# Key sums by head on either side of the array, the first k in two loads, and narrower first units, in a fused attention and expert kernel

The kernel runs on 1 core of one Trainium2 chip. The metric is the device time of one execution in microseconds (us); lower is better.

## The reference

```python
def phi(x):                                  # polynomial sketch, r = 8, so 64 features
    a = einsum('rd,bhsd->bhsr', S1, x); b = einsum('rd,bhsd->bhsr', S2, x)
    return einsum('bhsi,bhsj->bhsij', a, b).reshape(..., 64)
q_p, k_p = phi(q), phi(k)                    # batch 4, heads 4, seq 1088, head_dim 32
kv = einsum('bhsf,bhsd->bhfd', k_p, v); z = k_p.sum(axis=2)
attn = einsum('bhsf,bhfd->bhsd', q_p, kv) / (einsum('bhsf,bhf->bhs', q_p, z)[..., None] + 1e-6)
x = attn as 4352 rows of 128                 # heads side by side
p = domain_probs / (domain_probs.sum(-1) + 1e-9)
out = sum over 4 experts of p[:, e] * (relu(x @ w1[e]) @ w2[e])   # w1: 128 x 1024
```

## The kernel before

The expert product goes chunk by chunk over the rows: 16 steps a chunk, each with `first` (hidden block: TensorE, then ScalarE and VectorE) and, two steps later, `second` (TensorE). Attention work of later rows is cut into pieces and slipped between the steps; a unit is the number of query rows handled at once. Only the first 128 rows are handled ahead of everything, in `start`. A record is one matmul instruction of the trace. A PSUM tile is what a matmul of this program writes; `f`, `h`, `o`, `den` and `num` are such tiles. `den` and `num` are the products for the denominator and the numerator of the attention; their weights, `kvz`, are written by the key division from the key sums. To turn is to transpose.

```python
    UNITS = [[P, 480, 480]] + [[384, 352, 352]] * 3          # rows of a query unit, by batch
    CHUNKS = [P, 480, 480] + [512] * 5 + [320, 256, P]       # rows of an expert chunk
    ...
    def both(out, weights, moving, **flags):                 # the two 64-column sides of the array
        for _ in range(2):
            on_side(lambda s: out[half[s], :], lambda s: weights[:, half[s]], lambda s: moving, **flags)
    ...
    def key_sum(b, p, kv, t0=0, n=NT):                       # kv and z of a pair p of heads
        for t in range(t0, t0 + n):
            both(
                kv[:, 256 * p : 256 * p + 2 * (D + 1)],
                kps[b][:, t, p, :],                          # features of both heads: 128 columns
                vx[:, t, 2 * p : 2 * p + 2].rearrange("p h d -> p (h d)"),   # v and a 1, two heads: 66
                start=(p == t == 0), stop=(t == NT - 1), skip_group_check=True,
            )

    def key_divide(b, kv):                                   # zeroes the blocks of the wrong head
        kvz = apool.tile([P, 2, 2, HP], F32, tag="kvz", bufs=2, name="kvz")
        for i in (1, 0):                                     # 1: weights of den, 0: of num
            nc.vector.tensor_tensor(out=..., in0=_ap(kv, ...), in1=_ap(own2, ...), op=ALU.mult)
        kvzs[b] = kvz
    ...
    load_rows(k, 0, "kn")                                    # all 1088 columns in one load
    load_rows(q, 0, "qn", slice(0, P))
    ...
    for _ in range(14):                                      # warm-up matmuls
        wp = psum(ps_h, "h")
        nc.tensor.matmul(wp[:, :], warm[:, 0:P], warm[:, :], start=True, stop=True)
```

## Time and profile before

| | before |
|---|---|
| time, median of the first 3 runs | 501.05 us (500.58 to 501.96) |
| span of the profiled run | 499.2 us |
| TensorE busy, granted clock (share of the full TensorE clock) | 98%, 0.999 |
| first expert matmul | 15.49 us |
| from it to the first matmul of the last chunk | 464.22 us |

The lines of the profile on which the prediction rests stand in it, below.

### The profile page before, as it was taken

Reading aid. Unit: us, or ns where it says so; the run is one execution under the profiler, and the core shown is the slowest. Engines: PE = TensorE matmul, PEld = TensorE weight load, DVE = VectorE, ACT = ScalarE, POOL = GpSimd, SP = SyncE. Lnnn points to the kernel's source line nnn. Section 1 sums busy time; section 2 is a strip of 40 time slices with the busy share of each in tenths; the row PEclk is TensorE's granted clock in tenths of the full one; section 3 lists DMA queues with packets and bytes.
Section 4 is the critical chain, followed back from the end, with each engine's and each line's share of the span. In section 5 each row is a group of like instructions: output and inputs, shape, how many; then the busy total and the mean of one; then the engine's idle time right before and its main releaser. Section 6 shows DMA issues by size and latency. Waiting matters only on the chain.

```text
span 499.2 us, 11045 instructions
## 1 busy us (share of the span) xinstructions
PE 490.8 (98%) x4442; PEld 367.8 (74%) x4442; DVE 326.5 (65%) x749; ACT 250.7 (50%) x491; POOL 229.8 (46%) x264
## 2 busy tenths in 40 slices
PE   8899999999999999999999999999999999999997
PEld 6775788777776657777777777777777777788996
DVE  5858675868667585757657646558656557665643
ACT  4543553545454454544545455445455445556662
POOL 6730333444544263444545344344555355655571
PEclk9999999999999999999999999999999999999999
DMA  7981030021002330031001100021001100110000
GB/s 203 286 293 51 1 91 1 2 85 20 1 2 85 66 91 0 1 85 22 3 1 64 43 1 1 2 85 22 2 1 53 23 1 1 43 23 2 14 3 17
DMA packets 29666, 22.36 MB, mean 45 GB/s; under 512 B 20016, under 2 KB 26800, under 8 KB 29232
## 3 DMA queue, kind: packets, MB, share of 16 engines
q1 hardware_dynamic: 29312, 21.40, 15.3%
q8 instruction: 35, 0.57, 0.5%
q10 hardware_dynamic: 304, 0.26, 0.2%
q14 instruction: 15, 0.12, 0.1%
HBM read 19.35 MB, written 2.31 MB: 43 GB/s over the span
## 4 chain that ended last, share of the span: by engine, by line
PE 96%; DVE 3%; issue 0%; ACT 0%; DVEq 0%; ACTq 0%
PE h L186 48%; PE o L186 39%; PE f L186 5%; PE den L186 2%; PE num L186 1%; PE h L176 1%; DVE qp L420 1%; DVE hid L592 1%; DVE qa L479 0%; DVE qf L469 0%; DVE qb L474 0%; DVE qf L471 0%; DVE end L657 0%; ACT hid L618 0%; ACT fs L348 0%
## 5 line engine op out<-in xcount | busy, mean ns | idle before, releaser
L592 DVE SCALAR_TENSOR_TENSOR hid<-h,hid 128x256 f32<-128x256 f32 (+6 forms) x432 | 203.7, 472 | 149.0 <-ACT hid L618 140.7
L186 PE MATMUL h<-xT,w_sb 128*64 128x512 f32 (+4 forms) x1408 | 298.7, 496 | 1.7 <-DVE xT L454 1.4
L618 ACT ACTIVATE hid<-h 128x512 f32<-128x512 f32 (+3 forms) x288 | 158.3, 550 | 202.4 <-PE h L186 169.9
L186 PE MATMUL o<-hid,w2s 128*64 128x256 f32 (+3 forms) x1152 | 220.9, 355 | 0.0
L186 PEld LDWEIGHTS h<-xT,w_sb 128*64 128x64 f32 x1408 | 149.5, 137 | 52.7 <-issue 4.7
L186 PE MATMUL o<-hid,w_sb 128*64 128x256 f32 (+3 forms) x864 | 185.0, 356 | 0.6 <-DVE end L657 0.6
L186 PEld LDWEIGHTS o<-hid,w2s 128*64 128x64 f32 x1152 | 131.5, 137 | 31.7 <-issue 0.6
L733 POOL TENSOR_TENSOR ev<-yz,sh 64x256 f32<-64x256 f32 (+3 forms) x72 | 48.6, 675 | 159.0 <-ACT sh L736 156.3
L186 PEld LDWEIGHTS o<-hid,w_sb 128*64 128x64 f32 x864 | 101.4, 137 | 21.1 <-issue 1.6
L721 POOL TENSOR_TENSOR yz<-ev 128x512 f32<-128x512 f32 (+3 forms) x36 | 42.3, 1175 | 84.1 <-ACT ev L724 83.9
L733 POOL TENSOR_TENSOR ct<-ev 128x512 f32<-128x512 f32 (+3 forms) x36 | 42.2, 1173 | 2.8
L733 POOL TENSOR_TENSOR ct<-ct,gate 128x512 f32<-128x512 f32 (+3 forms) x27 | 31.9, 1183 | 2.1
L733 POOL TENSOR_TENSOR total<-total,ct 128x512 f32<-128x512 f32 (+3 forms) x27 | 31.8, 1177 | 2.1
L420 DVE TENSOR_TENSOR qp<-qa,qb 64x352 f32<-64x352 f32 (+2 forms) x44 | 31.6, 719 | 1.0
L610 ACT ACTIVATE hid<-h 128x256 f32<-128x256 f32 x24 | 15.3, 655 | 18.7 <-PE h L186 18.2
L723 ACT COPY ev<-o 128x512 f32<-128x512 f32 (+3 forms) x36 | 19.4, 538 | 9.4 <-PE o L186 8.9
L186 PE MATMUL o<-w_sb,hid 128*64 128x128 f32 x256 | 24.0, 273 | 0.0
L186 PEld LDWEIGHTS o<-w_sb,hid 128*64 128x64 f32 x256 | 19.9, 137 | 1.7 <-issue 1.5
L724 ACT COPY ev<-o 128x512 f32<-128x512 f32 (+3 forms) x36 | 19.4, 539 | 3.0
L359 DVE TENSOR_TENSOR kp<-fs 128x256 f32<-128x256 f32 (+1 forms) x24 | 16.1, 677 | 0.0
L736 ACT COPY sh<-yz 64x256 f32<-64x256 f32 (+3 forms) x36 | 13.7, 379 | 1.4 <-POOL yz L721 0.5
L737 ACT COPY sh<-yz 64x256 f32<-64x256 f32 (+3 forms) x36 | 13.7, 380 | 0.9
(93 smaller groups left out, 250.8 us busy)
## 6 DMA issues: line engine op xcount, KB each, us to landing
w_sb<-in_moe_w_dram SPq DMA_DIRECT2D x8, 512.0 KB, 7.7
gate<-gates SPq DMA_DIRECT2D x3, 1024.0 KB, 4.9
kn<-in_k_dram SPq DMA_DIRECT2D x4, 544.0 KB, 4.1
gate<-gates SPq DMA_DIRECT2D x2, 960.0 KB, 5.4
vn<-in_v_dram SPq DMA_DIRECT2D x14, 128.0 KB, 5.0
qn<-in_q_dram SPq DMA_DIRECT2D x3, 544.0 KB, 4.1
gate<-gates SPq DMA_DIRECT2D x1, 896.0 KB
out_dram<-ob SPq DMA_DIRECT2D x12, 64.0 KB, 2.0
```

The costliest lines, as they stand in the source:

```text
L186: nc.tensor.matmul(out(s), weights(s), moving(s), **flags)
L359: eng.tensor_tensor(out=_ap(kps[b], 0, P, 256 * t0 + P * p + 64 * x, [[256, n], [32, 2], [R, 4], [1, R]]), in0=in0, in1=_ap(fss[b], 0, P, ...
L420: nc.vector.tensor_tensor(out=qp[p][64 * x : 64 * x + 64, 0:n], in0=qa[64 * p : 64 * p + 64, 0:n], in1=qb[64 * p : 64 * p + 64, 0:n], op=A ...
L592: nc.vector.scalar_tensor_tensor(out=out, in0=src, scalar=0.0, in1=in1, op0=ALU.max, op1=ALU.subtract)
L610: nc.scalar.activation(turned, src, ACTF.Relu)
L618: nc.scalar.activation(hd[:, n * j : n * j + n], hp[:, 0:n], ACTF.Relu)
L721: add = lambda out, in0, in1, op=ALU.add: nc.gpsimd.tensor_tensor(out=out, in0=in0, in1=in1, op=op)
L723: nc.scalar.copy(_ap(ev, 0, P, 0, [[2 * w, 2], [1, w]]), _ap(a0, 0, P, 0, two))
L724: nc.scalar.copy(_ap(ev, 0, P, w, [[2 * w, 2], [1, w]]), _ap(a1, 0, P, 0, two))
L733: add = lambda out, in0, in1, op=ALU.add: nc.gpsimd.tensor_tensor(out=out, in0=in0, in1=in1, op=op)
L736: nc.scalar.copy(sh[HP:P, 0:w], yz[0:HP, 0, 0:w])
L737: nc.scalar.copy(sh[0:HP, 0:w], yz[HP:P, 1, 0:w])
```

## The change

The intent: a key sum computes only what is used (33 columns of one head on each side, instead of 66 of which half are zeroed); TensorE can start on the first half of k; the start has fewer sketch matmuls and warm-ups; and the first rows come in three units of 320, so that VectorE has less to do beside the first chunk.

```diff
-    QW = 480
+    QW = 384
-    UNITS = [[P, 480, 480]] + [[384, 352, 352]] * 3
+    UNITS = [[P, 320, 320, 320]] + [[384, 352, 352]] * 3
-    CHUNKS = [P, 480, 480] + [512] * 5 + [320, 256, P]
+    CHUNKS = [P, 320, 320, 320, 384] + [512] * 4 + [448, 256, P]
 ...
-    load_rows(k, 0, "kn")
+    kn[0] = lpool.tile([P, S], F32, tag="kn", bufs=2, name="kn")
+    for r in range(2):
+        nc.sync.dma_start(
+            _ap(kn[0], 0, P, P * r, [[8 * D, 4], [1, P]]),
+            bass.AP(k.tensor, k.offset + P * r, [[G * D, P], [8 * D, 4], [1, P]]),
+        )
     load_rows(q, 0, "qn", slice(0, P))
+    vn[0] = load_v(0, (nc.sync, nc.scalar), (0, 1))
+    load_rows(k, 0, "kn", slice(1024, S))
+    load_v(0, (nc.sync, nc.scalar), (2,), vn[0])
 ...
-    vn[0] = load_v(0, (nc.sync, nc.scalar))                  # stood a few lines further down
 ...
-    for _ in range(14):
+    for _ in range(11):
 ...            # key sketch: per head 16 columns; ScalarE's copies 8 -> 4; query sketch of the start 4 tiles -> 3
     def key_sum(b, p, kv, t0=0, n=NT):
         for t in range(t0, t0 + n):
-            both(
-                kv[:, 256 * p : 256 * p + 2 * (D + 1)],
-                kps[b][:, t, p, :],
-                vx[:, t, 2 * p : 2 * p + 2].rearrange("p h d -> p (h d)"),
+            for _ in range(2):
+                on_side(
+                    lambda s: kv[half[s], (D + 1) * p : (D + 1) * (p + 1)],
+                    lambda s: kps[b][:, t, p, half[s]],
+                    lambda s: vx[:, t, 2 * p + s],
 ...
     def key_divide(b, kv):
-        for i in (1, 0):
-            nc.vector.tensor_tensor(... own2 ...)
+        for i, copy in ((1, nc.vector.tensor_copy), (0, nc.scalar.copy)):
+            for h in range(2):
+                for x in range(2):
+                    copy(
+                        _ap(kvz[b % 2], 64 * x + 32 * h, 32, HP * i + D * h, [[P, 2], [1, D]]),
+                        _ap(kv, 64 * h + 32 * x, 32, D * i, [[D + 1, 2], [1 - i, D]]),
+                    )
 ...            # hidden blocks of the narrow chunks written straight instead of turned; the
                # gates' ends and the output of those chunks addressed row by row instead
-            if i:
+            if i > NQ // 2:
                 next(to_sum, None)
```

More of the change, by code (lines that the diff above doesn't have):

```diff
@@ L93, in load_rows, with load_v @@
         nc.sync.dma_start(d[b][:, part], bass.AP(src.tensor, src.offset + b * H * S * D + c, [[G * D, P], [1, n]]))
-    def load_v(b, engines):
-        t = lpool.tile([P, H * NT * D], F32, tag="vn", name="vn")
+    def load_v(b, engines, parts=(0, 1, 2), t=None):
+        t = t or lpool.tile([P, H * NT * D], F32, tag="vn", name="vn")
         base = v.offset + b * H * S * D
         for a in range(4):
-            engines[a // 2].dma_start(
-                _ap(t, 32 * a, 32, 0, [[8 * D, H], [1, 8 * D]]),
-                bass.AP(v.tensor, base + 8 * a * D, [[G * D, 32], [S * D, H], [1, 8 * D]]),
-            )
-        for a in range(2):
+            if a // 2 in parts:
+                engines[a // 2].dma_start(
+                    _ap(t, 32 * a, 32, 0, [[8 * D, H], [1, 8 * D]]),
+                    bass.AP(v.tensor, base + 8 * a * D, [[G * D, 32], [S * D, H], [1, 8 * D]]),
+                )
+        for a in range(2 if 2 in parts else 0):
             nc.sync.dma_start(
@@ L148 @@
         nc.sync.dma_start(
-            ends[:, i, :], bass.AP(domain_probs.tensor, domain_probs.offset + t * E, [[G * E, 32], [1, 4 * E]])
+            ends[:, i, :], bass.AP(domain_probs.tensor, domain_probs.offset + t * E, [[E, 4], [G * E, 32], [1, E]])
         )
@@ L154 @@
         load_w2(e)
-    own2 = cpool.tile([P, 2], F32, name="own2")
     sk = cpool.tile([P, P], F32, name="sk")
-    sp = cpool.tile([32, 4, HP], F32, name="sp")
-    sr = cpool.tile([P, 4, 2, P], F32, name="sr")
+    sp = cpool.tile([32, 3, 2, 32], F32, name="sp")
+    sr = cpool.tile([P, 3, 2, P], F32, name="sr")
     sq = cpool.tile([P, P], F32, name="sq")
@@ L163 @@
     nc.gpsimd.memset(sq[:, :], 0.0)
-    nc.gpsimd.memset(own2[:, :], 0.0)
-    for h in range(H):
-        nc.gpsimd.memset(own2[32 * h : 32 * h + 32, h % 2 : h % 2 + 1], 1.0)
     kT = cpool.tile([P, P * NT], F32, name="kT")
@@ L171 @@
     nc.gpsimd.memset(vx[64:P, NT - 1, :, 0:D], 0.0)
-    for _ in range(14):
+    kvz = [cpool.tile([P, 2, 2, HP], F32, name=f"kvz{i}") for i in range(2)]
+    for t in kvz:
+        nc.gpsimd.memset(t[:, :, :, :], 0.0)
+    for _ in range(11):
         wp = psum(ps_h, "h")
@@ L230 @@
     for h in range(H):
-        nc.scalar.copy(
-            _ap(sk, 32 * h, 32, R2 * (h // 2) + 4 * (h % 2), [[H * R2, 2], [R, 2], [1, 4]]),
-            _ap(s_T, 0, 32, 0, [[D, 2], [4, 2], [1, 4]]),
-        )
-        nc.scalar.copy(
-            _ap(sk, 32 * h, 32, H * R + R * h, [[H * R2, 2], [1, R]]), _ap(s_T, 0, 32, R, [[D, 2], [1, R]])
-        )
-    for i in range(2):
-        for j in range(2):
-            nc.gpsimd.tensor_copy(
-                _ap(sp, 0, 32, HP * (2 * i + j), [[32, 2], [R, 4], [1, R]]),
-                _ap(s_T, 0, 32, D * j, [[4, 2], [1, 4], [0, R]]) if i else _ap(s_T, 0, 32, D * j + R, [[0, 2], [0, 4], [1, R]]),
-            )
-    for h in range(H):
-        for i in range(2):
-            nc.gpsimd.tensor_copy(
-                _ap(sr, 32 * h, 32, P * (4 * i + 2 * (h // 2)) + 32 * (h % 2), [[P, 2], [HP, 2], [1, 32]]),
-                _ap(sp, 0, 32, P * i, [[HP, 2], [32, 2], [1, 32]]),
-            )
+        nc.scalar.copy(_ap(sk, 32 * h, 32, R2 * h, [[HP, 2], [1, R2]]), _ap(s_T, 0, 32, 0, [[D, 2], [1, R2]]))
+    for i in range(3):
+        nc.gpsimd.tensor_copy(
+            _ap(sp, 0, 32, HP * i, [[32, 2], [R, 4], [1, R]]),
+            _ap(s_T, 0, 32, 4 * (i - 1) if i else R, [[D, 2]] + ([[1, 4], [0, R]] if i else [[0, 4], [1, R]])),
+        )
+    for h in range(H):
+        nc.gpsimd.tensor_copy(
+            _ap(sr, 32 * h, 32, 32 * h, [[P, 6], [1, 32]]), _ap(sp, 0, 32, 0, [[32, 6], [1, 32]])
+        )
     mask_lo = [R2 + l % R2 for l in range(32)]
@@ L313 @@
     FG = ((0, 4), (4, 4), (8, 1))
-    fss, kps, kvzs = {}, {}, {}
+    fss, kps = {}, {}
     def key_turn(b, r):
@@ L336, in key_project @@
         if gi == 0:
-            fss[b] = apool.tile([P, 4, NT, R2], F32, tag="fs", name="fs")
+            fss[b] = apool.tile([P, 2, NT, 32], F32, tag="fs", name="fs")
             kps[b] = apool.tile([P, NT, 2, P], F32, tag="kp", name="kp")
@@ L340, in key_project @@
             for i in range(2):
-                both(
-                    kf[:, HP * t : HP * t + HP],
-                    kT[:, P * (t0 + t) : P * (t0 + t + 1)],
-                    sk[:, HP * i : HP * i + HP],
-                    start=(i == 0),
-                    stop=(i == 1),
-                )
+                for _ in range(2):
+                    on_side(
+                        lambda s: _ap(kf, HP * s, HP, 32 * t, [[P, 2], [1, 32]]),
+                        lambda s: kT[:, P * (t0 + t) + HP * s : P * (t0 + t) + HP * s + HP],
+                        lambda s: sk[:, HP * i : HP * i + HP],
+                        start=(i == 0),
+                        stop=(i == 1),
+                    )
         nc.scalar.copy(
-            _ap(fss[b], 0, P, R2 * t0, [[R2, n], [R2 * NT, 4], [1, R2]]),
-            _ap(kf, 0, P, 0, [[HP, n], [R2, 4], [1, R2]]),
+            _ap(fss[b], 0, P, 32 * t0, [[32 * NT, 2], [1, 32 * n]]), _ap(kf, 0, P, 0, [[P, 2], [1, 32 * n]])
         )
     def key_product(b, t0, n, p, x, eng, kf=None):
-        if kf is None:
-            in0 = _ap(fss[b], 0, P, R2 * (NT * p + t0) + R * x, [[R2, n], [4, 2], [1, 4], [0, R]])
-        else:
-            in0 = _ap(kf, 0, P, R2 * p + R * x, [[HP, n], [4, 2], [1, 4], [0, R]])
+        src, off = (kf, P * p) if kf is not None else (fss[b], 32 * (NT * p + t0))
         eng.tensor_tensor(
-            out=_ap(kps[b], 0, P, 256 * t0 + P * p + 64 * x, [[256, n], [32, 2], [R, 4], [1, R]]),
-            in0=in0,
-            in1=_ap(fss[b], 0, P, R2 * (NT * (2 + p) + t0), [[R2, n], [R, 2], [0, 4], [1, R]]),
+            out=_ap(kps[b], 0, P, 256 * t0 + P * p + 32 * x, [[256, n], [HP, 2], [R, 4], [1, R]]),
+            in0=_ap(src, 0, P, off + 4 * x, [[32, n], [R2, 2], [1, 4], [0, R]]),
+            in1=_ap(fss[b], 0, P, 32 * (NT * p + t0) + R, [[32, n], [R2, 2], [0, 4], [1, R]]),
             op=ALU.mult,
@@ L367, in key_sum @@
         for t in range(t0, t0 + n):
-            both(
-                kv[:, 256 * p : 256 * p + 2 * (D + 1)],
-                kps[b][:, t, p, :],
-                vx[:, t, 2 * p : 2 * p + 2].rearrange("p h d -> p (h d)"),
-                start=(p == t == 0),
-                stop=(t == NT - 1),
-                skip_group_check=True,
-            )
-    def key_divide(b, kv):
-        kvz = apool.tile([P, 2, 2, HP], F32, tag="kvz", bufs=2, name="kvz")
-        for i in (1, 0):
-            nc.vector.tensor_tensor(
-                out=_ap(kvz, 0, P, HP * i, [[P, 2], [D, 2], [1, D]]),
-                in0=_ap(kv, 0, P, D * i, [[256, 2], [D + 1, 2], [1 - i, D]]),
-                in1=_ap(own2, 0, P, 0, [[0, 2], [1, 2], [0, D]]),
-                op=ALU.mult,
-            )
-        kvzs[b] = kvz
+            for _ in range(2):
+                on_side(
+                    lambda s: kv[half[s], (D + 1) * p : (D + 1) * (p + 1)],
+                    lambda s: kps[b][:, t, p, half[s]],
+                    lambda s: vx[:, t, 2 * p + s],
+                    start=(p == t == 0),
+                    stop=(t == NT - 1),
+                    skip_group_check=True,
+                )
+    def key_divide(b, kv):
+        for i, copy in ((1, nc.vector.tensor_copy), (0, nc.scalar.copy)):
[4 more added lines that the diff above has]
+                        _ap(kv, 64 * h + 32 * x, 32, D * i, [[D + 1, 2], [1 - i, D]]),
+                    )
     def keys(b):
@@ L434, in attend @@
                     lambda s: nd[i][half[s], 0:n],
-                    lambda s: kvzs[b][:, s, 1 - i, :],
+                    lambda s: kvz[b % 2][:, s, 1 - i, :],
                     lambda s: qp[s][:, 0:n],
@@ L521, in start @@
             pass
-        fq = [psum(ps_o, "o0"), psum(ps_o, "o1")]
-        for i in range(2):
-            for p in range(2):
-                for j in range(2):
-                    both(fq[i][:, n * p : n * p + n], sr[:, 2 * i + p, j, :], qT[:, 0:n], start=(j == 0), stop=(j == 1))
+        fq = [psum(ps_o, "o0"), psum(ps_o, "o1"), psum(ps_n, "num")]
+        for i in range(3):
+            for j in range(2):
+                both(fq[i][:, 0:n], sr[:, i, j, :], qT[:, 0:n], start=(j == 0), stop=(j == 1))
         qb = apool.tile([P, QW], F32, tag="qb", name="qb")
-        nc.scalar.copy(qb[:, 0 : 2 * n], fq[0][:, 0 : 2 * n])
+        nc.scalar.copy(qb[:, 0:n], fq[0][:, 0:n])
         for x in range(2):
@@ L543, in start @@
         qp = query_tiles()
-        for p in range(2):
-            nc.vector.tensor_tensor(
-                out=qp[p][:, 0:n], in0=fq[1][:, n * p : n * p + n], in1=qb[:, n * p : n * p + n], op=ALU.mult
-            )
+        for x in range(2):
+            for p in range(2):
+                query_product(qp, p, x, n, fq[1 + x], qb)
         key_divide(b, kv)
@@ L603, in first @@
                 )
-            src = _ap(hp, 0, P, 0, [[n, 2], [32, n // 32], [1, 32]])
-            turned = _ap(hd, 0, P, 0, [[n, 2], [1, n // 32], [n // 32, 32]])
             if m and kq % 2:
-                nc.vector.tensor_scalar(out=turned, in0=src, scalar1=0.0, scalar2=None, op0=ALU.max)
+                nc.vector.tensor_scalar(
+                    out=hd[:, 0 : 2 * n], in0=hp[:, 0 : 2 * n], scalar1=0.0, scalar2=None, op0=ALU.max
+                )
             else:
-                nc.scalar.activation(turned, src, ACTF.Relu)
+                nc.scalar.activation(hd[:, 0 : 2 * n], hp[:, 0 : 2 * n], ACTF.Relu)
             work()
@@ L662, in second @@
                     nc.sync.dma_start(
-                        bass.AP(out.tensor, out.offset + t * DM, [[G * DM, 32], [1, 4 * DM]]), total.pop(m)[:, :]
+                        bass.AP(out.tensor, out.offset + t * DM, [[DM, 4], [G * DM, 32], [1, DM]]), total.pop(m)[:, :]
                     )
```

## The prediction

> **What bounds the kernel now.** I read the page first, then the chain that ended last in order of time for the first 46 us, then the timeline of the same stretch, and last the start times of the single matmul records. The page's first part and its slices:
>
> ```profile
> PE 490.8 (98%) x4442; PEld 367.8 (74%) x4442; DVE 326.5 (65%) x749; ACT 250.7 (50%) x491; POOL 229.8 (46%) x264
> ...
> PE   8899999999999999999999999999999999999997
> PEclk9999999999999999999999999999999999999999
> ...
> PE 96%; DVE 3%; issue 0%; ACT 0%; DVEq 0%; ACTq 0%
> ```
>
> TensorE is busy 98% of the span and is 96% of the chain, at the full clock. Only the first two slices (25 us) are below 9 tenths. So a change pays only if it takes work off TensorE or closes gaps in TensorE's stream; the 3% of the chain on VectorE say that some gaps are there. The chain shows where:
>
> ```profile
> 1.25 5.63 PE h L176 x14
> 6.88 2.25 PE h L186 x72
> 9.13 1.75 PE o L186 x32
> 10.88 2.15 PE f L186 x72
> ...
> 13.12 0.30 DVE kvz L382
> 13.47 0.46 PE den L186 x4
> ...
> 15.49 1.53 PE h L186 x24
> ...
> 20.93 0.35 DVE end L653
> 21.28 0.88 DVE qp L420
> ...
> 35.63 0.70 DVE qf L469
> 36.35 0.66 DVE qf L471
> ...
> 41.38 0.82 PE o L186 x5
> ```
>
> Columns: start, length, what. Read: 14 warm-up matmuls to 6.88, 72 key projections, 32 records of the first query's sketch, 72 key sums, then 2.4 us of short latencies to the first expert matmul at 15.49. Later two stretches belong to VectorE: 20.9 to 26.3 and 34.7 to 41.4.
>
> To size those gaps I use the trace's record starts. Back-to-back 512-column records start 215 ns apart, so a column costs 1/2.4 ns. Elapsed time from one chunk's first expert matmul to the next chunk's, less the columns of all records in between at that rate, is what was lost. For the chunks of 128, 480, 480, 512, 512, 512, 512, 512, 320 and 256 rows it is 1.91, 2.52, 0.47, 1.66, 0.47, 0.68, 0.69, 0.46, 0.41, 0.48 us. About 0.45 us is thus the floor for a chunk of some 350 records (1.3 ns a record), whatever its width. The excess sits in chunk 0 (about 1.5 us), chunk 1 (about 2.0 us) and chunk 3 (about 1.2 us). With the 15.5 us start, that is all that can be won.
>
> [...] with 64 moving columns (key projection) and with 66 (key sum), records of one side start 58.3 ns apart in both, and weight loads too. Were streaming the limit, 66 columns would take longer than 64. [...] here the first 11 warm-ups start 427 ns apart and the last ones about 217 ns, the change coming near 6.1 us. [...]
>
> ```profile
> L420 DVE TENSOR_TENSOR qp<-qa,qb 64x480 f32<-64x480 f32 x4 | 4.2, 1060 | 0.1
> 40.43 0.64 DVE L420 TENSOR_TENSOR qp<-qa,qb 64x480 f32<-64x480 f32 x1
> 22.71 1.15 POOL L502 TENSOR_TENSOR w2s<-w_sb 128x256 f32<-128x256 f32 x1
> 27.64 0.73 POOL L502 TENSOR_TENSOR w2s<-w2s,w_sb 128x256 f32<-128x256 f32 x1
> ```
>
> The first line is the groups of 20 to 27 us: 1060 ns for a product that takes 0.64 us at 40 us, when GpSimd is idle; GpSimd's sums take 1.15 instead of 0.73 us.
> [...] In the trace 512 B packets take 29 ns and k's 4352 B packets 220 ns, 26 ns per 512 B: k in pieces of 512 B costs little.
>
> **The change, part by part.**
>
> *Start, up to the first expert matmul.* The 11th warm-up ends its stream at 5.92, where the 12th starts. Key projection can start near 6.0, if k is turned. k's packets ran from 2.40 to 4.64 and it was used at 5.25; in halves, the first should be there near 4.0. VectorE ends the sketch's bit work at 4.73, so the first turn (0.67 us) goes from 4.75 instead of 5.25, the second ends near 6.1. ScalarE's sketch copies fall from 8 to 4 (about 0.1 us apart), done near 5.4. So projection moves by about 0.85 us, with no fewer records (36 matmuls of two records, 64 columns, as before). The small rest of k now comes after v on the same queue, perhaps at 7.4, in time for the third group at about 8.0, but not by much. Query sketch: 3 tiles x 2 parts x 2 sides x 2 records = 24 records for 32, at 54.7 ns: -0.44 us. Key sum: 72 records as before, 33 columns instead of 66, and each with a 64-column weight load: by the 58.3 ns above, **no gain**. Key division: two VectorE products (the first, 0.30 us, was enough for den) become four 32-partition copies on VectorE, and four on ScalarE beside them. Small ScalarE copies of that kind start 0.1 us apart and last 0.2; I take 0.5 to 0.55 us before den: +0.2 us. The sum is -0.85 -0.44 +0.2, about -1.1 us; first expert matmul near **14.4**.
>
> *Chunk 0.* The unit that runs beside it has 320 columns for 480. VectorE's work on it before was 14.8 us of nearly unbroken time (15.35 to 30.16); by the 352-column durations of the trace (0.53 turn, 0.55 shuffle, 0.51 product) 320 columns need about 11 us, against 15 us of TensorE work. den was asked for at 25.24 and waited for a product to 26.35; now it should not wait. [...] the weight sums come later in the program, but nothing before them on GpSimd waits for TensorE, so GpSimd still runs them at once. Of the 1.5 us I take 1.2: **-1.2 us**.
>
> *Chunk 1.* Its 2.0 us is the start of a wide chunk: two steps of LA are all the work TensorE has while ScalarE and VectorE handle the first hidden block, with 480-column attention work in between. At 320 columns both sides shrink by a third: **-0.7 us**.
>
> *One chunk more* (12 for 11): TensorE columns are the same in sum, another 350 records at the floor: **+0.45 us**.
>
> *Off the path.* Hidden blocks of the narrow chunks are written straight: ScalarE had 0.655 us against 0.384 us for 128x256 elsewhere, but its step was 0.87 us of TensorE work, so it bound nothing. At the end the last 23 output records run in one go from 494.3, so the last hidden block isn't waited for either. VectorE pays one unit more in fixed costs and 48 more hidden instructions, some 5 us of its 170 us of idle time. Key division in later batches is not waited for. I allow **-0.1 us** for all this.
>
> Sum: -1.1 -1.2 -0.7 +0.45 -0.1 = -2.65 us; 501.05 - 2.65 = **498.4 us**.
>
> **Rivals.**
> (a) *Narrow columns shorten the key sums.* If streaming were the limit, 288 records would save 33/2.4 = 13.75 ns each, 4.0 us in all, and the time would be near 494.5. Against it: 64 and 66 columns have the same 58.3 ns.
> (b) *VectorE becomes the early bound.* A 320-column step takes VectorE 324+486+324 = 1.13 us (rows of the 320 chunk) against 2.0 us of TensorE streaming, where 480 took 1.46 against 3.0: 57% for 49%. With some 31 us of attention work in chunks 1 to 3 (two units of 320, keys of batch 1, one of 384) I get 85 of 106 us, 80% (before: about 75%). Full bursts could then lose what chunk 1 wins; the time would be 499.5 to 500.5.
> (c) *The start does not move.* The third turn of k stands ahead of the first query's turn and the key products on VectorE; if k's rest lands past 8 us, projection ends late and some 0.7 us are lost again: about 499.1.
> (d) *Key division costs more*, 0.2 us a copy: +0.3 us.
>
> **Range and chances.** (b) and (c) together give 500.5; half of (a) with all gaps closed gives 495.5. Faster by over 2% would need 10 us, more than the start and all gaps yield. Slower by over 2% would need a new stall of 10 us, for which nothing speaks.
>
> **What would show it.** Records of the key sum still 58 ns apart on one side; key projection at 6.0; first expert matmul near 14.4; no wait of den for a product in chunk 0; lost time in chunk 0 below 0.8 us and in chunk 1 about 1.3. The prediction is wrong if key sums come at 30 ns a side pair, if TensorE waits for k's third turn, or if chunks 1 to 3 lose over 1 us each to VectorE.

The sum is -1.1 -1.2 -0.7 +0.45 -0.1 = -2.65 us, so 498.4 us. The 1.2 us of chunk 0 is the author's estimate, with VectorE's products beside GpSimd's sums as the trace has them (1.06 us, against 0.64 us at 40 us). That the sums are what slows these products is not shown.

## More of the kernel before

ScalarE's small copies in the start, from the timeline of that engine (start, length, engine, line, what):

```profile
4.83 0.20 ACT L231 COPY sk<-s_T 32x16 f32<-32x16 f32 x1 [1.75 <-DVE s_T L224]
4.94 0.20 ACT L235 COPY sk<-s_T 32x16 f32<-32x16 f32 x1
5.15 0.20 ACT L231 COPY sk<-s_T 32x16 f32<-32x16 f32 x1
5.26 0.20 ACT L235 COPY sk<-s_T 32x16 f32<-32x16 f32 x1
```

The two lines of one head, which write the same 32 partitions, start 0.11 us apart; from one head to the next, on other partitions, it is 0.21 us.

## The result, and the profile after

| | before | changed |
|---|---|---|
| median of 6 runs each | 500.81 us (500.37 to 502.29) | 502.41 us (502.03 to 504.03) |
| span of the profiled run | 499.2 us | 500.9 us |
| first expert matmul | 15.49 us | 16.62 us |
| from it to the first matmul of the last chunk | 464.22 us | 464.63 us |

The ratio is 1.0033, with a 95% interval of 1.0011 to 1.0055: a little slower, and outside the predicted range of 495.5 to 500.5. A ratio here is the mean time of one kernel's runs over that of the other's of the same rounds, so not quite the ratio of the two medians.

The chain that ended last in the changed kernel, first 17 us (start, length, what):

```profile
3.92 5.35 DMA kn<-in_k_dram
9.29 0.26 DVE kT L321
9.68 0.47 PE h L194 x8
...
13.63 0.21 DVE kvz L381
13.85 0.22 DVE kvz L381
14.08 0.22 DVE kvz L381
14.31 0.24 DVE kvz L381
14.60 0.46 PE den L194 x4
...
16.61 1.53 PE h L194 x24
```

Before, the chain in this stretch was TensorE from 1.25 to 13.0. Now it goes through a load of k until 9.27, and the key division has four links, 0.92 us instead of 0.30. VectorE's timeline of the same stretch shows the waits in brackets:

```profile
5.56 0.71 DVE L316 STREAM_TRANSPOSE kT<-kn 128x512 f32<-128x512 f32 x1 [0.91 <-DMA kn<-in_k_dram]
7.51 0.71 DVE L316 STREAM_TRANSPOSE kT<-kn 128x512 f32<-128x512 f32 x1 [1.24 <-DMA kn<-in_k_dram]
9.29 0.24 DVE L321 STREAM_TRANSPOSE kT<-kn 128x64 f32<-128x64 f32 x1 [1.07 <-DMA kn<-in_k_dram]
```

All three turns of k wait for their data; the second half came at 7.5 us, where the whole of k had come at 5.25 before.

Further on, one stretch of the changed kernel stands out. ScalarE's and VectorE's timelines, 316 to 322 us, in the chunk with the last key division:

```profile
317.22 1.15 DVE L585 SCALAR_TENSOR_TENSOR hid<-h,hid 128x512 f32<-128x512 f32 x2 [1.43 <-ACT hid L610]
318.28 0.91 DVE L381 COPY kvz<-f 32x64 f32<-32x64 f32 x4
319.23 0.85 ACT L381 COPY kvz<-f 32x64 f32<-32x64 f32 x4 [2.04 <-DVE kvz L381]
320.10 0.58 ACT L715 COPY ev<-o 128x512 f32<-128x512 f32 x1
321.06 1.11 ACT L610 ACTIVATE hid<-h 128x512 f32<-128x512 f32 x2
321.71 0.42 DVE L585 SCALAR_TENSOR_TENSOR hid<-h,hid 128x256 f32<-128x256 f32 x1 [2.51 <-ACT hid L610]
```

ScalarE stood idle for 2.04 us ahead of its four copies, until VectorE had done its own four, and only then went on to the blocks that TensorE needs.

From the starts of the matmul records I take, as in the prediction, the time from one chunk's first expert matmul to the next chunk's. For the changed kernel these lengths are 15.56, 34.09, 38.70, 35.08, 42.36, 57.03, 55.53, 58.90, 53.42, 46.80, 27.16 us. What is telling: in the traces of kernels that differ only in the start (changed and e1_k_whole, for example) they come out the same to 0.05 us. Only the start varies, by some tenths, and the first chunk, by the clock. So a single trace tells the effect of an edit on a chunk far more finely than the times do.

### The profile page after: what moved, and what is told of

Read it like the earlier page. It is cut to its first block, busy times and chain, and to the rows that moved or that the text cites. A ratio compares the mean times of both kernels' runs of the same rounds, so it can differ in the third digit from the quotient of the medians.

```text
span 500.9 us, 11963 instructions
## 1 busy us (share of the span) xinstructions
PE 489.7 (98%) x4795; PEld 339.2 (68%) x4795; DVE 328.6 (66%) x827; ACT 250.8 (50%) x551; POOL 233.3 (47%) x279
## 4 chain that ended last, share of the span: by engine, by line
PE 94%; DVE 2%; DMA 1%; ACT 1%; POOL 1%; issue 1%; SPq 0%; DVEq 0%; ACTq 0%; POOLq 0%
PE h L194 47%; PE o L194 40%; PE f L194 4%; PE den L194 2%; PE num L194 1%; DMA kn<-in_k_dram 1%; DVE hid L585 1%; ACT hid L610 0%; DVE kvz L381 0%; SPq L133 0%; SPq L100 0%; POOL sq L545 0%; POOL kp L355 0%; ACT kvz L381 0%; DVE end L649 0%
## 5 line engine op out<-in xcount | busy, mean ns | idle before, releaser
L585 DVE SCALAR_TENSOR_TENSOR hid<-h,hid 128x256 f32<-128x256 f32 (+8 forms) x480 | 210.3, 439 | 146.1 <-ACT hid L610 136.3
L194 PE MATMUL h<-xT,w_sb 128*64 128x512 f32 (+5 forms) x1536 | 301.3, 468 | 1.2 <-DVE xT L450 0.6
L610 ACT ACTIVATE hid<-h 128x512 f32<-128x512 f32 (+4 forms) x320 | 163.2, 512 | 198.0 <-PE h L194 159.1
L194 PE MATMUL o<-hid,w2s 128*64 128x256 f32 (+4 forms) x1280 | 232.7, 337 | 0.0
L194 PE MATMUL o<-hid,w_sb 128*64 128x256 f32 (+4 forms) x960 | 181.2, 337 | 1.4 <-ACT ev L715 0.9
L725 POOL TENSOR_TENSOR ev<-yz,sh 64x256 f32<-64x256 f32 (+4 forms) x80 | 50.6, 632 | 162.3 <-ACT sh L728 159.3
L713 POOL TENSOR_TENSOR yz<-ev 128x512 f32<-128x512 f32 (+4 forms) x40 | 43.3, 1084 | 75.0 <-ACT ev L716 74.7
L725 POOL TENSOR_TENSOR ct<-ev 128x512 f32<-128x512 f32 (+4 forms) x40 | 43.3, 1083 | 3.1
L725 POOL TENSOR_TENSOR total<-total,ct 128x512 f32<-128x512 f32 (+4 forms) x30 | 32.5, 1082 | 2.4
L715 ACT COPY ev<-o 128x512 f32<-128x512 f32 (+4 forms) x40 | 19.9, 498 | 8.7 <-PE o L194 7.5
L716 ACT COPY ev<-o 128x512 f32<-128x512 f32 (+4 forms) x40 | 20.2, 505 | 0.1
```

Of the source, the lines that this page charges most:

```text
L194: nc.tensor.matmul(out(s), weights(s), moving(s), **flags)
L585: nc.vector.scalar_tensor_tensor(out=out, in0=src, scalar=0.0, in1=in1, op0=ALU.max, op1=ALU.subtract)
L610: nc.scalar.activation(hd[:, n * j : n * j + n], hp[:, 0:n], ACTF.Relu)
L713: add = lambda out, in0, in1, op=ALU.add: nc.gpsimd.tensor_tensor(out=out, in0=in0, in1=in1, op=op)
L715: nc.scalar.copy(_ap(ev, 0, P, 0, [[2 * w, 2], [1, w]]), _ap(a0, 0, P, 0, two))
L716: nc.scalar.copy(_ap(ev, 0, P, w, [[2 * w, 2], [1, w]]), _ap(a1, 0, P, 0, two))
```

## Experiments

**The two groups of runs.** All full runs fall in two groups. Split at a mean granted clock of 0.998, the kernel before has a median of 500.92 us (24 runs) above and 502.05 (16 runs) below, in the rounds of the experiments; the changed kernel 502.12 (4) and 503.89 (2). The first group is what the parts below are compared in; the ratios given are of all runs.

**e1_k_whole** - the changed kernel with k loaded whole.

```diff
-    (two loads of 512 B pieces, and the rest behind v)
+    load_rows(k, 0, "kn")
     load_rows(q, 0, "qn", slice(0, P))
```

> The changed kernel with the first k loaded whole again (one load of 4352 B pieces ahead of q and v, no piece behind v). Theory A (512 B pieces of k land late and hold TensorE): k usable near 5.2 us instead of 5.6 and 7.5, its rest with it instead of 9.3; key projection from about 6.0 without a gap; first expert matmul near 14.7 instead of 16.6 us, the whole run about 1.9 us shorter than the changed kernel, about 500.5. Rival B (the start is set by the key division and GpSimd, not by k): first expert matmul stays within 0.3 us of 16.6.

Measured: 501.36 us, ratio 1.0 (0.9988 to 1.0012); first expert matmul at 15.24 instead of 16.62; all later lengths as in the changed kernel. The direction is theory A's, the size less: 1.4 of 1.9 us in the traces, and 0.8 us by the times at the full clock (502.12 and 501.36). k came at 5.58, not at 5.25, and the key division took its 0.92 us here too. The packets show what else lay in the way. Whole, k's 128 packets of 4352 B started between 2.25 and 4.75 us; in pieces of 512 B they went on until 6.3 us. Between 2.5 and 3.5 us the 16 DMA engines were 0.37 to 0.85 busy (0.55 to 0.99 with k whole), and from 3.75 us on they were full in both. But from 3.25 to 4.0 and again from 4.75 to 5.5 us a third to three fifths of them was taken by v, which ScalarE's queue had asked for at 1.57 us in both kernels: all 256 of those packets of 1024 B started before k in pieces was done, 50 of them before k whole was. And a packet of 512 B took 27 ns in the median, one of 4352 B 168 ns, that is 20 ns per 512 B. No run moved v out of the way, so how much of the delay is v's and how much the pieces' own is not shown.

**e10_k_rest_early** - the changed kernel with the last piece of k ahead of q and v.

```diff
+    load_rows(k, 0, "kn", slice(1024, S))
     load_rows(q, 0, "qn", slice(0, P))
     vn[0] = load_v(0, (nc.sync, nc.scalar), (0, 1))
-    load_rows(k, 0, "kn", slice(1024, S))
```

> The changed kernel with the last small piece of k loaded right after the two halves, ahead of q and v. If the order (piece behind v) held the start: first expert matmul 1 us or more earlier than 16.6. If the 512 B pieces did: the second half is still usable only near 7.5 us, TensorE still waits for it, and the first expert matmul comes within 0.6 us of 16.6.

Measured: 503.61 us (1.0031, 1.001 to 1.0051; four of six runs in the low-clock group); first expert matmul at 15.64; second half used at 6.92, third piece at 7.55, TensorE waiting 0.5 us. It lies between the two expectations. The start of unchanged programs varies, though: the changed kernel, e2_kvz_apart and e4_sum_66 have the same start and show 16.62, 16.21 and 15.98 us; k whole (e1, e3, e5) 15.24, 15.47, 15.46. By means, halves cost 0.9 us, and the early rest wins back about 0.6 of it. Both the pieces and the order count; the split between them is not settled by one trace.

**e2_kvz_apart** - the changed kernel with the two axes of `kvz` exchanged.

```diff
-    _ap(kvz[b % 2], 64 * x + 32 * h, 32, HP * i + D * h, [[P, 2], [1, D]]),
+    _ap(kvz[b % 2], 64 * x + 32 * h, 32, P * i + D * h, [[HP, 2], [1, D]]),
```

> The changed kernel with the two axes of the kvz tile exchanged, so that VectorE's copies and ScalarE's copies write separate stretches of columns. Theory A (ScalarE's four copies wait for VectorE's four only because their columns lie interleaved, and block ScalarE's queue): the two groups of copies run side by side, ScalarE's do not start after VectorE's end; the loss in the chunks with a key division (2.7, 1.9 and 3.0 us) falls by 0.5 to 1.5 us each; the whole run 1.5 to 3 us shorter. Rival B (the wait is for the last key sum in both): nothing changes, within 0.5 us of the changed kernel.

Measured: 502.98 us (1.0038, 1.0022 to 1.0054); every length as in the changed kernel, ScalarE's copies still after VectorE's. My theory A fell; but rival B, that both wait for the sum, does not fit either, for ScalarE starts when VectorE ends: at 14.25 us in the first key division, where VectorE's four took from 13.22 to 14.14.

**e3_both** - both edits.

> Both edits at once. If the two causes are separate, the gains add: some 3.5 to 5 us below the changed kernel, near 498, which would be under the kernel before. If they share the same wait, no more than the larger of the two.

Measured: 501.7 us (1.0013, 0.9999 to 1.0027), start at 15.47, lengths unchanged: what e1 brought, and nothing from the other.

**e4_sum_66** - 66 moving columns again, only that.

```diff
-    lambda s: vx[:, t, 2 * p + s],
+    lambda s: vx[:, t, 2 * p : 2 * p + 2].rearrange("p h d -> p (h d)"),
```

> The changed kernel with 66 moving columns in each key sum instead of 33 (the other head's sums are made and not read; the result stays right). Theory (weight loads of 64 columns set the pace at 58 ns a side): 72 records still take 2.05 us from first start to last, and the time is within 0.5 us of the changed kernel. Rival (columns are streamed at 1/2.4 ns): 288 records of 13.75 ns more, 4 us longer.

Measured: 503.28 us (1.0038, 1.0022 to 1.0054; four of six runs at the low clock, the others at 502.15 against the changed kernel's 502.12). The groups of matmuls by shape, changed kernel and then e4_sum_66 (count, busy us, mean ns):

```profile
L194 PE MATMUL f<-vx,kp 128*64 128x33 f32 x288 | 10.1, 222 | 0.0
```

```profile
L194 PE MATMUL f<-vx,kp 128*64 128x66 f32 x288 | 10.3, 222 | 0.0
```

All chunk lengths but the first agree to 0.01 us. Half the columns saved nothing: 72 records took 2.05 us from first to last start before and after the change, and 2.08 here. The mean of 222 ns is no pace: with 72 starts within 2.05 us, the records overlap, and the pace is seen in the starts only. What sets the pace is not shown by this: 66 columns at 1/2.4 ns (from 215 ns for 512) are 27.5 ns, still under the 29 ns from one record to the next, and every narrow record here loads 64 weight columns, so a weight load and any other fixed cost of a record would look alike.

**e5_kvz_tiles, e6_kvz_dve, e7_kvz_act, e8_keys_before** - all on e1_k_whole: two tiles for the two groups of copies; all eight on VectorE; all eight on ScalarE; the whole keys' part of the kernel before.

```diff
-    kvz = [cpool.tile([P, 2, 2, HP], ...) for i in range(2)]                       # e5
+    kvz = [[cpool.tile([P, 2, HP], ...) for i in range(2)] for b in range(2)]
-    for i, copy in ((1, nc.vector.tensor_copy), (0, nc.scalar.copy)):
+    for i, copy in ((1, nc.vector.tensor_copy), (0, nc.vector.tensor_copy)):       # e6
+    for i, copy in ((1, nc.scalar.copy), (0, nc.scalar.copy)):                     # e7
```

> e1_k_whole (first k whole) with VectorE's and ScalarE's copies of the key division writing two different tiles. Theory C (the wait of ScalarE's copies comes from writing the same tile): ScalarE's copies start within 0.2 us of VectorE's, the three chunks with a key division (38.70, 57.03 and 58.90 us in e1_k_whole) get 0.5 to 1.5 us shorter each. Rival D (the wait comes from reading the same PSUM tile on two engines): ScalarE's copies still start after VectorE's last one, chunks unchanged within 0.1 us.

> e1_k_whole with all eight copies of the key division on VectorE. If the loss is ScalarE's queue standing behind VectorE: the three chunks get shorter, by 0.5 to 1.5 us each, though VectorE has 0.85 us more to do; the start gets no longer than 0.2 us. If the loss is VectorE's own time: the three chunks get longer.

> e1_k_whole with all eight copies on ScalarE, which then waits for the key sum alone. If ScalarE's wait for VectorE is the loss: the three chunks get shorter by 0.5 to 1.5 us each. If ScalarE's 1.7 us of small copies are the loss whoever it waits for: about unchanged.

> e1_k_whole with the keys' part of the kernel before (sketch layout, products, sums of 66 columns, division by two products with a mask on VectorE); row partition, query sketch and hidden layout stay changed. If the eight copies cost what the two traces suggest: the three chunks 0.5 to 1.5 us shorter each and the first expert matmul 0.6 us earlier, the whole run near 498.5. If the keys' part is not the cause: within 0.5 us of e1_k_whole.

Measured, with the lengths of the three chunks that hold a key division:

| kernel | median us | ratio (interval) | first expert matmul | the three chunks | their sum |
|---|---|---|---|---|---|
| changed | 502.41 | 1.0033 (1.0011 to 1.0055) | 16.62 | 38.70, 57.03, 58.90 | 154.63 |
| e5, two tiles | 502.37 | 1.0025 (0.9998 to 1.0053) | 15.46 | 38.70, 57.03, 58.90 | 154.63 |
| e6, all VectorE | 499.87 | 0.9976 (0.9952 to 1.0) | 15.94 | 38.29, 56.68, 57.51 | 152.48 |
| e7, all ScalarE | 499.45 | 0.9965 (0.9942 to 0.9989) | 15.07 | 38.22, 56.69, 57.60 | 152.51 |
| e8, keys of before | 499.56 | 0.9963 (0.9933 to 0.9994) | 14.60 | 37.88, 56.78, 57.51 | 152.17 |

Separate tiles change nothing, so it isn't the written tile that makes ScalarE wait. Eight copies on either engine alone cost little; it is splitting them that costs 2.1 us. With the old keys the three chunks are 2.46 us shorter than in the changed kernel. Not all of what was expected came: of the 0.5 to 1.5 us for each chunk, only the third kept to it in all three kernels; the second gave 0.25 to 0.35, the first 0.41 to 0.82. And e6 was to lengthen the start by no more than 0.2 us; its 15.94 us is 0.5 to 0.7 more than with k whole (15.24 to 15.47). In e8 the same stretch of VectorE's timeline reads:

```profile
314.07 1.15 DVE L588 SCALAR_TENSOR_TENSOR hid<-h,hid 128x512 f32<-128x512 f32 x2 [1.43 <-ACT hid L613]
315.14 0.48 DVE L381 TENSOR_TENSOR kvz<-f,own 128x128 f32<-128x128 f32 x2
316.53 0.42 DVE L588 SCALAR_TENSOR_TENSOR hid<-h,hid 128x256 f32<-128x256 f32 x1 [0.91 <-ACT hid L613]
```

VectorE is back at the hidden blocks 2.46 us after it began the previous ones (314.07 to 316.53); in the changed kernel, 4.49 us (317.22 to 321.71).

**e13_two_sums** - e5_kvz_tiles with the key sums made twice, in two PSUM tiles, one for each engine.

```diff
-    kv = psum(ps_f, "f")
+    kv = [psum(ps_n, "den"), psum(ps_f, "f")]      # key_sum into both; copies of i read kv[i]
```

> e5_kvz_tiles (separate tiles written) with the key sums made twice, in two PSUM tiles, one read by VectorE and one by ScalarE; 288 more records, some 8 us longer. If the wait comes from reading one PSUM tile on two engines: ScalarE's copies now start without VectorE's, at the end of the sums, in the first key division within 0.3 us of VectorE's. If they still start after VectorE's last copy, the wait has another cause, such as the program order of the two groups.

Measured: 507.44 us, one run. The first key division, from the two engines' timelines of this run and of e5_kvz_tiles:

```profile
13.92 0.84 ACT L375 COPY kvz<-den 32x64 f32<-32x64 f32 x4 [3.57 <-PE den L188]
14.52 0.92 DVE L375 COPY kvz<-f 32x64 f32<-32x64 f32 x4 [2.53 <-PE f L188]
```

```profile
12.46 0.92 DVE L375 COPY kvz<-f 32x64 f32<-32x64 f32 x4 [0.65 <-POOL dsum L254]
13.50 0.85 ACT L375 COPY kvz<-f 32x64 f32<-32x64 f32 x4 [3.30 <-DVE kvz L375]
```

With a PSUM tile of its own ScalarE starts when its sums are made, 0.6 us ahead of VectorE, whose sums end later. In the other three key divisions of this run, too, ScalarE never waits for VectorE's copies; in e5_kvz_tiles it waits for them in all four, 7.9 us in sum. The three chunks took 158.47 us; less three times the 2.1 us of the 72 added records that is 152.2 us (an estimate), what e8 takes. So, by these two runs, the wait is for the other engine's reads of the same PSUM tile; by what mechanism, they do not show. (The "POOL dsum" of the second fence is the inferred releaser that came last by the profile; the copies read `f`, which TensorE had just ended.)

**e9_rows_only** - the kernel before with the rows' partition of the change alone (`QW`, `UNITS`, `CHUNKS`).

> The kernel before with the rows' partition of the change alone (units 128 and three of 320, twelve chunks, tiles of 384). If the partition is what shortened chunks 0 and 1: from the first expert matmul to the first of the last chunk it takes what e8_keys_before takes (462.1 us), about 2 us under the kernel before (464.2), with the start at 15.5; the time about 1.5 to 2 us below before. If the hidden layout and the later weight sums did it: within 0.5 us of before, or longer by the 0.45 us of one chunk more.

Measured: 499.54 us, 0.996 (0.994 to 0.9979). Its lengths are those of e8_keys_before to 0.01 us from the second chunk on. The first is 17.43 instead of 15.56 us, for its trace fell in the low-clock group. Putting 15.56 in its place, the stretch to the last chunk is 463.99 - 1.87 = 462.12 us, against 464.22 before: the partition is worth 2.1 us, and neither the hidden layout nor the later weight sums show in any chunk. What the low clock is, the table of stretches shows, from e9_rows_only (stretch, its length, busy us of the five engines, granted clock, DMA share, GB/s):

```profile
14.00:16.00 2.00, 0.64 (x12) 0.54 (x12) 1.79 (x7) 0.00 (x0) 0.50 (x1) 1.00 1.10 330
16.00:18.00 2.00, 2.00 (x24) 1.69 (x20) 1.39 (x5) 1.64 (x3) 1.42 (x4) 0.60 1.08 356
18.00:20.00 2.00, 2.00 (x20) 1.72 (x18) 1.35 (x5) 0.10 (x1) 2.00 (x3) 0.54 1.17 329
20.00:22.00 2.00, 2.00 (x42) 2.00 (x40) 0.82 (x4) 1.38 (x3) 1.92 (x4) 1.00 1.07 344
```

Just after the stretch in which TensorE is busy for 0.64 of 2.00 us, its granted clock is 0.60 and 0.54: 20 records instead of 42 in 2 us. Together these two stretches lack what half the clock for some 3.5 us would take (an estimate from the two figures). All three traces of the low group show such a fall (17 to 19 us: 0.53 in e4, 0.50 in e9 and e10), and 45 of the 103 runs with a clock on record, e12 and e13 left out, were in that group. In e9 TensorE's idle times of 0.49 and 1.36 us, with 0.66 us of matmuls between them, came just before the fall. But the trace of the kernel before has the same two, ahead of 13.47 and of 15.49 us, and a clock of 1.00 from 14 to 22 us. That they cause the fall is not shown.

**e11_keys_before_again** - e8_keys_before with more rounds.

> e8_keys_before once more with five rounds, as the best version so far: about 0.4% below the kernel before, with the same chunk lengths as in e8_keys_before to 0.1 us; only the start may differ, by some tenths.

Measured: 499.59 us, 0.9973 (0.9946 to 1.0001), lengths as before to 0.01 us, start at 14.73. Three runs at the full clock gave 498.47 us in the median, three at the low one 500.99: the times of six runs could not tell what the trace told.

**e12_kept_warm** - the best version: e8_keys_before, with six warm-up matmuls in the start where TensorE was idle.

```diff
+        keep_warm(1)
         key_divide(b, kv)
-        for _ in attend(b, 0, n, qp):
-            pass
+        for j, _ in enumerate(attend(b, 0, n, qp)):
+            if j == 0:
+                keep_warm(5)
```

> e8_keys_before with one warm-up matmul after the first key sums and five after the first num, in time in which TensorE stood idle. The fast runs so far fall into two groups, of granted clock 1.0 and about 0.996, some 1.9 us apart, and a trace of the second kind has clock 0.5 from 16.5 to 20 us. If TensorE's idle time ahead of the first expert matmul lets the clock fall: no run of this kernel has a clock under 0.998, all runs lie within 0.5 us near the best of e8 (spans of 496.4), and the median is 498.3 or so against 499.6. If the fall has another cause: again about half the runs 1.9 us longer. If the warm-ups delay den: the start is later by up to 0.3 us.

Measured: 498.48 us (498.23 to 499.07), **0.9945 (0.9927 to 0.9963)**: under both kernels. All six runs have a clock of 0.999 or 1.0, while four of the eleven runs of the kernel before beside them were at 0.997. That fits the theory but does not show it: it is six runs, and e1_k_whole, without these warm-ups, had five of five at the full clock, where e5_kvz_tiles, with nearly the same start, had two of four. The six spread over 0.84 us, not 0.5. The start was later than hoped, 15.06 us, 0.3 to 0.5 more than in e8 and e11, as the first expert matmul now waited until 14.96 and not for `xT` alone; why is not looked into.

```profile
12.00:14.00 2.00, 1.86 (x20) 0.97 (x16) 1.25 (x6) 0.00 (x0) 0.44 (x2) 1.00 1.10 353
14.00:16.00 2.00, 1.44 (x21) 0.97 (x21) 1.77 (x8) 0.25 (x1) 0.00 (x0) 1.00 1.05 350
16.00:18.00 2.00, 2.00 (x36) 1.78 (x33) 0.78 (x3) 0.91 (x3) 1.59 (x3) 1.00 1.12 342
```

From 12 to 16 us TensorE is busy 3.30 us, where e8_keys_before has 0.78 + 1.41 = 2.19, and the clock stays at 1.00. It did so in the traces of e8 and e11 too, so the trace alone proves nothing.

## Why the prediction was wrong

The prediction was 498.4 us, 2.65 below before; the change came out slower. By the sum's own terms, from the traces:

| term | predicted | measured | from |
|---|---|---|---|
| start without the key division and with k on time | -0.85 -0.44 = -1.29 | -0.89 | e8 (14.60) against before (15.49) |
| key division in the start | +0.2 | +0.64, with the rest of the keys' part | e1 (15.24) against e8 (14.60) |
| k in halves | 0 | +1.38 in these traces, +0.9 by means | changed (16.62) against e1 (15.24) |
| rows: chunks 0 and 1, one chunk more | -1.2 -0.7 +0.45 = -1.45 | -2.1 | e9 against before |
| key division in later batches | 0 ("is not waited for") | +2.5 | changed (464.63) against e8 (462.11) |
| end, from the last chunk's first matmul | -0.1 | +0.2 | 19.62 against 19.44 us |
| sum | -2.65 | +1.7 | spans 500.9 and 499.2 |

The rows of the start rest on single traces, whose starts vary by some tenths.

**The step that failed most** is the half sentence "Key division in later batches is not waited for". For VectorE alone it would have been nearly true: with all eight copies there (e6), the three chunks take 152.48 us, against 152.17 with the old keys (e8). I had looked at the two groups of copies as work "beside" each other and asked only what waits for kvz. But both read one PSUM tile, ScalarE's copies waited for VectorE's (2.04 us in the stretch shown), and VectorE's came after its own hidden blocks (317.22 and 318.28 us). ScalarE ran nothing else meanwhile, nor the hidden blocks that feed TensorE: the four matmuls of the next one had ended by 318.96 us in the trace, and ScalarE began it at 321.06 us, after its copies. Of the 2.5 us, 2.1 went when one engine made all the copies (e6, e7). That reading one PSUM tile is what kept the two engines apart is shown by e5 and e13: the copies went one group after the other with one tile, and overlapped with two. No run here shows what would happen with one tile and the two not kept apart.

**The second** is "k in pieces of 512 B costs little". The prediction set a mean of 220 ns for the 4352 B packets, drawn up by the slow first ones (the first took 835 ns), against 29 ns for 512 B and found no difference; the medians are 168 ns, or 20 ns per 512 B, and 27 ns. And it looked at k alone, where v's packets were to share the engines. The halves came at 5.5 and 7.5 us instead of near 4.0 and by 5.4, and key projection began at 6.42, not 6.0. Rival (c) had the small rest of k past 8 us; it came at 9.3.

**The third** is "Small ScalarE copies of that kind start 0.1 us apart". In the trace before, that held only for copies to the same partitions; from one group of 32 partitions to another it was 0.21 us, and each of the copies in question changes the group. In the changed kernel ScalarE's copies, each to another group than the one before, start 0.21 to 0.23 us apart and last 0.20 to 0.22. The copies to the same group differ in form from each other, so no run shows that the group alone decides. VectorE's four took 0.92 us ahead of den, not 0.5 to 0.55: +0.64 instead of +0.2. Rival (d) put it at 0.3.

What held: the key sum's columns are worth nothing (e4), by the pace of about 58 ns a side; the wait of den in chunk 0 is gone, with 0.79 us lost there instead of 1.91; chunk 1 loses 1.34 us instead of 2.52, and the rows' partition brought more than I allowed; VectorE did not become the bound (rival b). A small miss at the end: the output of the last 128 rows, now addressed row by row, had its 512 B packets start over 0.88 us instead of 0.32, and the last of them 2.12 us after the load's issue instead of 1.56, which ate what the shorter tail of matmuls had won.

The prediction also had no word on a fall of the clock after the start. TensorE is idle for 2.2 us between the key sums and the first expert matmul, against 1.9 us before, and runs of the low-clock group came with both (2 of 6; 16 of 40 before). That the idle time brings them on is not shown; runs of that group are some 1.1 us (before) to 2.5 us (e11) longer, which is as much as the terms in dispute.

## What to carry to other kernels

When work is split between two engines, ask what they read as well as what they write: here ScalarE's copies from a PSUM tile that VectorE read too came after VectorE's (e5: 13.50 us, where VectorE had begun at 12.46), and with a tile of its own beside them (e13: 13.92 and 14.52); the split cost 2.1 us over three key divisions of eight copies of 32x64, and ScalarE's next hidden blocks came after its copies. A shorter moving operand saved nothing where the records kept one pace, here about 58 ns a side for 33, 64 and 66 columns. And where a schedule is static, compare stretch lengths of two traces before comparing times: here those after the first chunk repeat to 0.05 us, while the times of one program spread over 2 us.
